# Weights transposed back in 32x32 blocks by VectorE, and plain transfers in place of DMA transposes, in an agent-attention kernel with a gated convolution

## The chip, the core and the metric

The kernel runs on one core of a Trainium2 chip. The metric is the device time of one execution in microseconds. Five engines work side by side, each with its own queue of instructions in program order: TensorE (PE, with weight loads as PEld), VectorE (DVE), ScalarE (ACT), GpSimd (POOL) and SyncE (SP), which here issues nearly all transfers. The transfers run on 16 DMA engines.

## What is computed

For each of 4 batches q, k and v are 12,800 x 128 and there are 49 agents of 128. Two softmaxes compose into an attention, and a gated causal convolution with two projections follows:

```
def sm(a, b):
    s = scale * (a @ b.transpose(0, 2, 1))
    s = s - s.max(-1, keepdims=True)
    e = np.exp(s)
    return e / (e.sum(-1, keepdims=True) + 1e-09)
a2k = sm(agents, k)
agent_v = a2k @ v
q2a = sm(q, agents)
x = q2a @ agent_v
...
for k in range(K):                       # K = 5 taps, causal
    gate_pre += conv_w[k][None, None, :] * xp[:, k:k + S, :]
gate = 1.0 / (1.0 + np.exp(-gate_pre))
val = x @ w_val
return (gate * val @ w_out).astype(np.float32)
```

## The kernel before

The attention's result x is never formed. Since x is the 49 weights of a position (q2a) times the 49 rows of agent_v, the kernel folds agent_v into the convolution's taps and into w_val once for each batch (`fold_weights`), and the gate and the value then are matmuls over the 49 weights of a position and its four predecessors. The weights and the folded matrices are each split into a high and a low half-precision part; the products high x high, high x low and low x high need 49 x 3 = 147 rows of contraction. 128 of them form the tile x1 (low, high and 30 agents' high once more), and the 19 that are left, for each of 5 taps, form the 95 rows of x2.

The work is cut into units of 1,280 positions: 10 a batch, 40 in all, and for the convolution into 100 chunks of 512 positions (the last is cut into 384 and 128). The steps are named by letters:

- k (`key_scores`, L406): scores of a unit of keys against the agents, 8 matmuls of 320 columns, a copy to ks, a running maximum.
- v (`agent_values`, L475): the exponentials, their 32x32 block transposes on VectorE (L400), and the product with v, added up in PSUM over the 10 units of a batch.
- max and fold: the maximum over a batch's keys (L433), and the folded weights (L527), in 2 and 5 pieces.
- q (`queries`, L743): scores of a unit of queries, block transposes into sT (L400), maximum (L757), subtraction (L762), exponential (L770), sum (L775), division (L783). The weights w of a unit lie in qw with 128 positions on the partitions, 10 blocks of 49 agents. They are split into pt (10 blocks of 128 columns): high by a cast on ACT (L790), 30 high ones copied once more by POOL in two strided pieces (L796), low by a subtraction on POOL (L804).
- t (`transposes`, L837): pt has positions on its partitions, x1 needs them along its free dimension. For the first 4 units PE transposes 10 blocks and ACT and DVE copy them out (L859 to L871). For the other 36, one DMA transpose a unit does it (L845). Then `shifts` (L876) fills x2 by plain transfers from x1: each row of x1 is copied to 5 rows of x2, shifted by one position each. From unit 4 on this is done once for a pair of units, in two transfers by `X2CUTS` (L37): 16 rows of x1 (50, 53, ...) to 80 rows of x2, and 3 rows to 15 (L894). `halo` (L823) copies four columns between segments on POOL.
- g, a, o (`gates` L908, `values` L952, `project` L991): for each chunk 6 matmuls for the gate (L932 over x1, L936 over x2) and tanh, 2 for the value (L959, L963) and the product with the gate, and 3 for the projection (L1004 to L1006), scaled on ACT and sent out by pairs of chunks (L1040).

Buffers: 11 load slots for k, q and v (NLOAD), 4 tiles of pt, 4 of x1 with one pair of units each, 3 of x2, one PSUM bank each for gate, value and projection.

The order on PE is written out by hand (`order`, L1107). All other engines, SP among them, follow a planner (`Plan`, L70): each step has an engine, a cost in us, and, for a transfer, the time that it takes of the wire; the planner runs the steps in a model and emits them in the order of their start. Loads are held back to 20 us ahead of their use. A step waits by keys that it reads and writes, such as ("pt", 2, 0) or ("x1", 1, 0). A transfer that waits holds up every later one on SP.

Of the kernel before, what the change touches and what calls it, by code (L numbers as in the profile page):

```python
# [9 lines left out]
F32 = mybir.dt.float32  # L10
F16 = mybir.dt.float16
# [6 lines left out]
P = 128  # L18
G = 4
# [13 lines left out]
NDUP = 30  # L33
THIRDS = 16
X2R = 19
LAST = 42
X2CUTS = ((0, THIRDS, 1, 3, 0.5), (THIRDS, X2R, LAST, 3, 0.2))  # L37
# [4 lines left out]
NPT = 4  # L42
NX = 4
# [147 lines left out]
def tile_agent_attention_gated_conv(  # L191
# [37 lines left out]
    sts = ring(2, [P, NBLK, AP_], F32, "sT")  # L229
    qmx = ring(2, [P, NBLK], F32, "qmx")  # L230
# [3 lines left out]
    pts = ring(NPT, [P, NBLK, P], F16, "pt")  # L234
# [198 lines left out]
    def key_max(b):  # L433
# [16 lines left out]
        def spread():  # L450
            nc.vector.tensor_reduce(
                out=mrow, in_=p1[0:2, 0:P].rearrange("j (g a) -> j a g", g=G),
                axis=AX.X, op=ALU.max,
            )
            nc.vector.tensor_copy(
                out=mrep, in_=mrow.unsqueeze(1).to_broadcast([2, G, BLK])
            )

        add("dve", 0.5, spread, [at1], ["mrep"])
# [67 lines left out]
    def fold_weights(b):  # L527
# [58 lines left out]
        ghi = wst[:, 0:TAPS, 0:A]  # L586
        vhi = wst[:, TAPS, 0:A]

        def thirds(x, first, end):
            return x[..., first:end:3]  # L590

        def lows(low, full, hi, less):


            for out, first, end in zip(low, (2, 0, 1, LAST), (A, LAST, A, A)):
                less(out, thirds(full, first, end), thirds(hi, first, end))

        def rest(out, full, s, hi):
            dve.scalar_tensor_tensor(
                out=out, in0=full, scalar=rs[:, s : s + 1], in1=hi,  # L600
                op0=ALU.mult, op1=ALU.subtract,
            )

        def val_weights():
# [9 lines left out]
            dve.tensor_scalar_mul(vhi, pv[:, 0:A], rs[:, 1:2])  # L614
            low = (
                wst[:, TAPS, 2 * A : 2 * A + THIRDS], wst[:, TAPS, 2 * A + THIRDS :],
                x2v[:, HALO, 0:THIRDS], x2v[:, HALO, THIRDS:],
            )
            lows(low, pv[:, 0:A], vhi, lambda out, full, hi: rest(out, full, 1, hi))

        gate_lows = (
            wst[:, 0:TAPS, 2 * A : 2 * A + THIRDS], wst[:, 0:TAPS, 2 * A + THIRDS :],
            x2g[:, :, 0:THIRDS], x2g[:, :, THIRDS:],
        )

        def gate_weights():
            dve.tensor_scalar_mul(ghi, gw, rs[:, 0:1])
# [6 lines left out]
        def gate_rest_pool():  # L634
# [3 lines left out]
            lows(gate_lows, gs, ghi, less)  # L638

        def gate_rest():  # L640
            lows(gate_lows, gw, ghi, lambda out, full, hi: rest(out, full, 0, hi))
# [9 lines left out]
        add("dve", 1.58, val_weights, [at_v], [(*w_, "v"), "mxv"])  # L651
        add(
            "act", 0.4,
            lambda: nc.scalar.copy(out=wst[:, 0:TAPS, A : 2 * A], in_=ghi),
            [(*w_, "g")], [(*w_, "d")],
        )
        add(
            "act", 0.22, lambda: nc.scalar.copy(out=wst[:, TAPS, A : 2 * A], in_=vhi),
            [(*w_, "v")], [(*w_, "e")],
        )  # L660
        if b:
            add("dve", 0.95, gate_rest, ["gw", (*w_, "g")], [(*w_, "r")])
# [4 lines left out]
        def transposes():  # L667
# [6 lines left out]
            "pe", 0.6, transposes, [(*w_, n) for n in "derv"] + [(*w_, "g")], [at_w],  # L674
# [530 lines left out]
```

## Time and profile before

| | us |
|---|---|
| median of 3 runs | 418.15 |
| lowest and highest | 415.93, 419.5 |
| the profiled execution, its own time | 415.52 |
| its span, first to last instruction | 413.4 |

| engine | busy us | share | instructions |
|---|---|---|---|
| PE | 395.0 | 96% | 3905 |
| DVE | 256.0 | 62% | 489 |
| ACT | 297.8 | 72% | 519 |
| POOL | 282.1 | 68% | 381 |

A busy share is an average over the whole span. A row of a group names its line, engine and operation, what it writes and reads, then its count, its busy time and the mean of one. A row of the transfers names what is written from what, the engine that issues, how often, the size of one (KB are 1,024 bytes here) and the median time from issue to landing, where it is known. The share of the DMA engines is the time that their packets took, over 16 engines; it can pass 1, since a packet's time counts in the window in which it starts. The GB/s count each packet once.

### The profile page before, as it was taken

Reading aid. Unit: us, or ns where it says so; the run is one execution under the profiler, and the core shown is the slowest. Engines: PE = TensorE matmul, PEld = TensorE weight load, DVE = VectorE, ACT = ScalarE, POOL = GpSimd, SP = SyncE. Lnnn points to the kernel's source line nnn. Section 1 sums busy time; section 2 is a strip of 40 time slices with the busy share of each in tenths; the row PEclk is TensorE's granted clock in tenths of the full one; section 3 lists DMA queues with packets and bytes.
Section 4 is the critical chain, followed back from the end, with each engine's and each line's share of the span. In section 5 each row is a group of like instructions: output and inputs, shape, how many; then the busy total and the mean of one; then the engine's idle time right before and its main releaser. Section 6 shows DMA issues by size and latency. Waiting matters only on the chain.

```text
span 413.4 us, 10115 instructions
## 1 busy us (share of the span) xinstructions
PE 395.0 (96%) x3905; PEld 197.1 (48%) x3905; DVE 256.0 (62%) x489; ACT 297.8 (72%) x519; POOL 282.1 (68%) x381
## 2 busy tenths in 40 slices
PE   4859999999999999999999999999999999999996
PEld 2348544445555434445446544445465544444443
DVE  3758688854835857566745687576664697643231
ACT  2564568597884777869885677689886676888875
POOL 1003679766878698656788775896578789998752
PEclk9969999999999999999999999999999999999999
DMA  8999999999999999999999999999999999999933
GB/s 323 420 416 411 366 360 357 284 358 252 350 320 267 336 269 317 337 306 330 346 356 296 298 347 311 340 303 342 310 348 313 261 302 291 223 251 232 216 144 138
DMA packets 75130, 127.63 MB, mean 309 GB/s; under 512 B 50466, under 2 KB 50850, under 8 KB 75084
## 3 DMA queue, kind: packets, MB, share of 16 engines
q1 hardware_dynamic: 74940, 126.87, 99.9%
q8 instruction: 30, 0.49, 0.5%
q10 hardware_dynamic: 144, 0.13, 0.2%
q14 instruction: 16, 0.13, 0.1%
HBM read 79.25 MB, written 26.21 MB: 255 GB/s over the span
## 4 chain that ended last, share of the span: by engine, by line
PE 85%; DMA 7%; ACT 3%; DVE 3%; POOL 1%; issue 1%; SPq 0%; DVEq 0%; ACTq 0%
PE gate L932 25%; PE sc L390 17%; PE av L494 11%; PE out L1004 5%; PE val L959 5%; PE gate L936 5%; PE val L963 5%; PE out L1005 5%; PE out L1006 5%; DMA ld<-kT 4%; DMA x<-x 2%; ACT e L485 1%; ACT th L945 1%; PE sc L859 1%; DVE h L972 0%
## 5 line engine op out<-in xcount | busy, mean ns | idle before, releaser
L985 POOL TENSOR_TENSOR hl<-h,hh 128x512 f16<-128x512 f32 x99 | 114.6, 1160 | 57.4 <-ACT hh L980 55.0
L932 PE MATMUL gate<-x,stat 128*128 128x512 f16 (+1 forms) x500 | 124.3, 378 | 0.6 <-ACT e L485 0.4
L972 DVE SCALAR_TENSOR_TENSOR h<-th,val 128x512 f32<-128x512 f32 x100 | 68.1, 681 | 81.6 <-PE out L1005 27.8
L390 PE MATMUL sc<-ld,ag_sb 128*32 128x320 f32 x1280 | 97.1, 442 | 7.5 <-DMA ld<-kT 6.3
L1025 ACT ACTIVATE ob<-out,oscale 128x512 f32<-128x512 f32 x98 | 67.2, 686 | 23.4 <-PE out L1006 23.3
L945 ACT ACTIVATE th<-gate,unscale 128x512 f32<-128x512 f32 x100 | 68.5, 685 | 21.3 <-PE gate L936 19.2
L932 PEld LDWEIGHTS <-stat 128*128 128x128 f16 x505 | 47.7, 97 | 60.6 <-issue 5.5
L980 ACT CAST hh<-h 128x512 f16<-128x512 f32 x99 | 60.7, 613 | 14.4 <-DVE h L972 13.8
L762 POOL TENSOR_TENSOR qw<-sT,qmx 128x490 f32<-128x490 f32 x40 | 40.5, 1018 | 43.8 <-DVE qmx L757 41.3
L390 PEld LDWEIGHTS sc<-ld,ag_sb 128*32 128x32 f32 x1280 | 37.9, 111 | 54.9 <-issue 17.4
L494 PE MATMUL av<-ld,eT 128*32 128x129 f32 (+1 forms) x1400 | 50.5, 277 | 2.2 <-DVE eT L400 2.2
L494 PEld LDWEIGHTS av<-ld,eT 128*32 128x32 f32 (+1 forms) x1400 | 45.6, 115 | 10.3 <-issue 3.4
L416 ACT COPY ks<-sc 128x640 f32<-128x640 f32 x40 | 27.6, 693 | 27.3 <-PE sc L390 25.1
L400 DVE STREAM_TRANSPOSE sT<-sc 128x640 f32<-128x640 f32 x40 | 33.5, 842 | 19.9 <-PE sc L390 19.1
L400 DVE STREAM_TRANSPOSE eT<-e 128x640 f32<-128x640 f32 x40 | 33.5, 839 | 19.1 <-ACT e L485 11.2
L804 POOL TENSOR_TENSOR pt<-qw,pt 128x490 f16<-128x490 f32 x40 | 43.9, 1104 | 1.9 <-ACT pt L790 1.8
L485 ACT ACTIVATE e<-ks,kbias 128x320 f32<-128x320 f32 x80 | 39.4, 554 | 7.4 <-DVE eT L400 4.6
L783 POOL TENSOR_TENSOR qw<-qw,qr 128x490 f32<-128x490 f32 x40 | 40.3, 1009 | 3.3
L936 PE MATMUL gate<-x,stat 95*128 95x512 f16 x100 | 38.0, 380 | 0.8 <-DMA x<-x 0.8
L959 PE MATMUL val<-x,stat 128*128 128x512 f16 x100 | 38.0, 380 | 0.1
L425 DVE TENSOR_REDUCE kmx<-ks 128x2 f32<-128x640 f32 x39 | 31.5, 811 | 10.5 <-ACT ks L416 10.5
L963 PE MATMUL val<-x,stat 95*128 95x512 f16 x100 | 38.0, 380 | 0.0
(133 smaller groups left out, 407.7 us busy)
## 6 DMA issues: line engine op xcount, KB each, us to landing
ld<-kT SPq DMA_DIRECT2D x40, 640.0 KB, 7.0
ld<-qT SPq DMA_DIRECT2D x40, 640.0 KB, 9.1
ld<-vP SPq DMA_DIRECT2D x39, 645.0 KB, 6.5
outT<-ob SPq DMA_DIRECT2D x48, 512.0 KB, 7.2
x<-x SPq DMA_DIRECT2D x18, 400.0 KB, 5.2
x<-x SPq DMA_DIRECT2D x18, 75.0 KB
x<-x SPq DMA_DIRECT2D x4, 200.0 KB
outT<-ob SPq DMA_DIRECT2D x3, 256.0 KB
```

Source lines behind the costliest of these rows:

```text
L390: nc.tensor.matmul(out=out[g * BLK : (g + 1) * BLK, j, 0:GT], lhsT=ag_sb[:, b, j * BLK : (j + 1) * BLK], rhs=src[:, g * GT : (g + 1) * GT] ...
L400: nc.vector.transpose(out=out.rearrange("p n (j i) -> p j n i", j=2), in_=in_.rearrange("p j (n i) -> p j n i", i=BLK),)
L494: nc.tensor.matmul(out=av[o + j : o + j + cols, 0 : C + 1], lhsT=et[:, n, j : j + cols], rhs=vt[:, n, :], start=(u == 0 and n < 2), stop=( ...
L932: nc.tensor.matmul(out=pg, lhsT=stat[:, k, :], rhs=x1[:, c : c + w], start=(k == 0), stop=False,)
L936: nc.tensor.matmul(out=pg, lhsT=stat[0 : TAPS * X2R, TAPS + 1, :], rhs=x2[0 : TAPS * X2R, o2 : o2 + w], start=False, stop=True,)
L945: lambda: nc.scalar.activation(out=th, in_=pg, func=AF.Tanh, scale=unscale[:, 0:1]),
L959: nc.tensor.matmul(out=pv, lhsT=stat[:, TAPS, :], rhs=x1s[(b * NCH + n0 // CH) // 5 % NX][:, PAD + o2 : PAD + o2 + w], start=True, stop=False,
L963: nc.tensor.matmul(out=pv, lhsT=stat[0 : TAPS * X2R, TAPS + 2, :], rhs=x2[0 : TAPS * X2R, o2 : o2 + w], start=False, stop=True,)
L972: lambda: nc.vector.scalar_tensor_tensor(out=h, in0=th, scalar=1.0, in1=pv, op0=ALU.add, op1=ALU.mult),
L980: "act", 0.18 + 0.43 * scale, lambda: nc.scalar.copy(out=hh, in_=h),
L985: lambda: nc.gpsimd.tensor_tensor(out=hl, in0=h, in1=hh, op=ALU.subtract),
L1025: lambda: nc.scalar.activation(out=ob[:, o : o + w], in_=po, func=AF.Copy, scale=oscale if w == CH else 1.0),
```

## The change

Weights are no longer split with positions on the partitions. VectorE first transposes w back in 32x32 blocks (`back`): two overlapping groups of 32 agents, 0 to 31 and 17 to 48 (SLOT = 17), 640 elements a partition into the new tile wT, in which a partition is one of 32 agents in one of four strips of positions. ACT casts wT to the high parts and POOL subtracts, both 640 wide, into the tile pr, which holds four kinds of rows (low, high, high, low) for a pair of units. Then `strips` moves pr to x1 by plain transfers, eight for a pair of units: for each of the four strips of 32 partitions one transfer of 30 partitions with 3 rows each to 90 rows of x1, and one of 19 partitions with 2 rows each to 38 rows. A row has 640 elements of 2 bytes. The host lays q out so that each strip is a run of 640 positions. The first four units stay on PE, with pt now lying inside pr.

x1's rows are so ordered anew (triples for 30 agents, pairs for 19), and the folded weights follow (`highs`, `lows`): for all batches the gate's splits are now on ACT and POOL, where before this held for batch 0 and the others had them on DVE. x2 takes other rows: `X2CUTS` now sends 17 rows of x1 to 85 rows of x2 and 2 rows to 10. The copy of the keys' maximum and the unscaling go from DVE to ACT. The hand-written order on PE is new; its start is shown, and the number of steps of each kind is the same.

```
-NDUP = 30
-THIRDS = 16
+SLOT = 17
+AFIRST = 30
 X2R = 19
-LAST = 42
-X2CUTS = ((0, THIRDS, 1, 3, 0.5), (THIRDS, X2R, LAST, 3, 0.2))
+X2CUTS = ((0, SLOT, 1, 3, 0.5), (SLOT, X2R, 124, 2, 0.2))
...
+NPR = 2
...
+    wts = ring(2, [P, 2, GT], F32, "wT")
...
-    pts = ring(NPT, [P, NBLK, P], F16, "pt")
+    prs = ring(NPR, [P, 4, 2 * GT], F16, "pr")
...
-        add("dve", 0.5, spread, [at1], ["mrep"])
+            ),
+            [at1], ["mrow"],
+        )
+        add(
+            "act", 0.25,
...
+        def highs(i, full, copy):
+            for out, agents in (
+                (wst[:, i, 0 : 3 * AFIRST].rearrange("p (a k) -> p a k", k=3)[:, :, 0:2], full[:, 0:AFIRST]),
+                (wst[:, i, 3 * AFIRST :].rearrange("p (a k) -> p a k", k=2), full[:, AFIRST:]),
+            ):
+                copy(out, agents.unsqueeze(2).to_broadcast([P, agents.shape[1], 2]))
+
+        def lows(x2, k, full, less):
+
+
+            one, two = wst[:, k, 0 : 3 * AFIRST : 3], wst[:, k, 3 * AFIRST :: 2]
+            for out, first, end in (
+                (wst[:, k, 2 : 2 + 3 * (AFIRST - SLOT) : 3], SLOT, AFIRST),
+                (wst[:, k, 2 + 3 * (AFIRST - SLOT) : 3 * AFIRST : 3], AFIRST, A - 2),
+                (x2[..., 0:SLOT], 0, SLOT), (x2[..., SLOT:], A - 2, A),
+            ):
+                hi = one[..., first:end] if end <= AFIRST else two[..., first - AFIRST : end - AFIRST]
+                less(out, full[..., first:end], hi)
...
-        if b == 0:
-            add("pool", 0.47, gate_scaled, ["gw", "rsg"], ["gs"])
-            add("act", 0.4, lambda: nc.scalar.copy(out=ghi, in_=gs), ["gs"], [(*w_, "g")])
-            add("pool", 1.27, gate_rest_pool, ["gs", (*w_, "g")], [(*w_, "r")])
-        else:
-            add("dve", 0.47, gate_weights, ["gw", "rsg"], [(*w_, "g")])
...
+        add("pool", 0.47, gate_scaled, ["gw", "rsg"], ["gs"])
+        add(
+            "act", 0.4,
+            lambda: nc.scalar.copy(
+                out=wst[:, 0:TAPS, 0 : 3 * AFIRST].rearrange("p t (a k) -> p t a k", k=3)[..., 0:2],
+                in_=gs[:, :, 0:AFIRST].unsqueeze(3).to_broadcast([P, TAPS, AFIRST, 2]),
+            ),
+            ["gs"], [(*w_, "g")],
+        )
+        add(
+            "act", 0.35,
+            lambda: nc.scalar.copy(
+                out=wst[:, 0:TAPS, 3 * AFIRST :].rearrange("p t (a k) -> p t a k", k=2),
+                in_=gs[:, :, AFIRST:].unsqueeze(3).to_broadcast([P, TAPS, A - AFIRST, 2]),
+            ),
+            ["gs"], [(*w_, "d")],
+        )
+        add("pool", 1.27, gate_rest, ["gs", (*w_, "g"), (*w_, "d")], [(*w_, "r")])
...
-        add("dve", 0.15, unscales_, ["mxg", "mxv"], [("unscale", x)])
+        add(
+            "act", 0.22,
...
+        if on_pe(b, u):
+            pt = blocks(g)
...
+            p_ = [("pr", i_, k, n) for k in (2 * h, 2 * h + 1) for n in range(2)]
+            add("act", 0.8, high, [("qw", g % NPT)], [p_[0]])
+            add("pool", 0.7, again, [("qw", g % NPT)], [p_[1], p_[2]])
+            add("pool", 1.3, low, [("qw", g % NPT), p_[0]], [p_[3]])
...
+        pr = prs[i_][:, :, h * GT : (h + 1) * GT]
+        wT = wts[x]
+
+        def back():
+            pairs = [summed.ap[0], summed.ap[1], (SLOT, 2), (1, BLK)]
+            nc.vector.transpose(
+                out=wT.rearrange("p j (n i) -> p n j i", i=BLK),
+                in_=bass.AP(summed.tensor, summed.offset, pairs),
+            )
+
+        add("dve", 0.83, back, [("qw", g % NPT)], [("wT", x)])
+        add(
+            "act", 0.69, lambda: nc.scalar.copy(out=pr[:, 1:3], in_=wT),
+            [("wT", x)], [("pr", i_, k, h) for k in (1, 2)],
+        )
+        add(
+            "pool", 1.43,
             lambda: nc.gpsimd.tensor_tensor(
-                out=pt[:, :, 0:A], in0=w, in1=pt[:, :, A : 2 * A], op=ALU.subtract
-            ),
-            [("qw", g % NPT), (*p_, 0)], [(*p_, 1)],
-        )
+                out=pr[:, 0::3], in0=wT, in1=pr[:, 1:3], op=ALU.subtract
+            ),
+            [("wT", x)] + [("pr", i_, k, h) for k in (1, 2)], [("pr", i_, k, h) for k in (0, 3)],
...
-        return [(x, i, h) for h in halves for x in ("x1", "x1b")] + [("x1h", i)] * (0 in halves)
+        return [(x, i, h) for h in halves for x in ROWS] + [("x1h", i)] * (0 in halves)
...
+    ROWS = ("x1", "x1b", "x1c", "x1d")
+
+    def strips(g):
+
+
+        i, s = g // 2 % NPR, g // 2 % NX
+        pr, x1 = prs[i], x1s[s]
+        step = pr.ap[0][0]
+        for part, (slots, a0, a1, row) in enumerate(
+            (((0, 1, 2), 0, AFIRST, 0), ((2, 3), AFIRST - SLOT, BLK, 3 * AFIRST))
+        ):
+            n, rows = len(slots), len(slots) * (a1 - a0)
+            for strip in range(G):
+                src = pr[strip * BLK + a0 : strip * BLK + a1, slots[0] : slots[-1] + 1]
+                dst = x1[row : row + rows, PAD + strip * 2 * GT : PAD + (strip + 1) * 2 * GT]
+                add(
+                    "dma", 0.6,
+                    lambda src=src, dst=dst: nc.sync.dma_start(out=dst, in_=src),
+                    [("pr", i, k, h) for k in slots for h in range(2)],
+                    [(ROWS[2 * part + strip % 2], s, strip // 2)], rows * 0.0053,
+                )
...
-            dst = unit_rows(g)
-            add(
-                "dma", 1.4,
-                lambda: nc.sync.dma_start_transpose(
-                    out=dst.rearrange("p (n i) -> p n i", i=P),
-                    in_=pt.rearrange("p n r -> p (n r)"),
-                ),
-                [(*p_, n) for n in range(3)], [("x1", g // 2 % NX, g % 2)], 2.4,
-            )
-            shifts(b, u)
+            if g % 2:
+                strips(g)
+                shifts(b, u)
...
-            first += A
...
-        "k0.4 k0.1 k0.7 k0.9 k0.5 k0.0 k0.8 k0.6 k0.2 k0.3 m0 m0 v0.0 v0.1 v0.2 q0.0 v0.3 v0.4 "
-        "v0.5 v0.6 q0.1 v0.7 v0.8 v0.9 f0 t0.0 f0 k1.2 k1.0 k1.4 q0.2 f0 k1.3 f0 t0.1 g0 f0 q0.3 "
...
+        "k0.4 k0.0 k0.3 k0.1 k0.8 k0.2 k0.6 k0.5 k0.7 k0.9 m0 m0 q0.0 v0.0 v0.1 v0.2 v0.3 v0.4 "
+        "v0.5 v0.6 v0.7 v0.8 q0.1 v0.9 k1.4 t0.0 f0 k1.2 f0 q0.2 k1.3 k1.0 f0 t0.1 f0 g0 a0 q0.3 "
+        "q0.5 f0 g1 o0 k1.5 k1.1 a1 t0.2 g2 t0.4 a2 q0.4 t0.3 g3 o1 a3 g4 a4 o2 t0.5 q0.7 q0.6 o3 "
...
+    qT = np.ascontiguousarray(
+        q.reshape(b, nu // 2, G, 2, GT, c).transpose(0, 5, 1, 3, 2, 4).reshape(b, c, n)
+    )
```

More of the change, by code (lines that the diff above doesn't have):

```diff
@@ L585, in fold_weights, with rest @@
         x2v = wst[:, TAPS + 2, 0 : TAPS * X2R].rearrange("p (r k) -> p k r", k=TAPS)
[L586 to L598, printed above, removed]
+        def highs(i, full, copy):
[13 more added lines that the diff above has]
+                less(out, full[..., first:end], hi)
+        def rest(out, full, hi):
             dve.scalar_tensor_tensor(
-                out=out, in0=full, scalar=rs[:, s : s + 1], in1=hi,
+                out=out, in0=full, scalar=rs[:, 1:2], in1=hi,
                 op0=ALU.mult, op1=ALU.subtract,
@@ L613, in val_weights @@
             dve.reciprocal(out=rs[:, 1:2], in_=mx[:, 1:2])
[L614 to L627, printed above, removed]
+            highs(TAPS, pv[:, 0:A], lambda out, full: dve.tensor_scalar_mul(out, full, rs[:, 1:2]))
+            lows(x2v[:, HALO], TAPS, pv[:, 0:A], rest)
         def gate_scaled():
@@ L673, in fold_weights @@
         add(
-            "pe", 0.6, transposes, [(*w_, n) for n in "derv"] + [(*w_, "g")], [at_w],
+            "pe", 0.6, transposes, [(*w_, n) for n in "dgrv"], [at_w],
             key="m",
@@ L787, in queries, with high, again @@
         add("pool", 1.29, weigh, [("qw", g % NPT), ("qr", x)], [("qw", g % NPT), ("qr", x)])
-        p_ = ("pt", g % NPT)
-        add(
-            "act", 0.6, lambda: nc.scalar.copy(out=pt[:, :, A : 2 * A], in_=w),
-            [("qw", g % NPT)], [(*p_, 0)],
-        )
-        def again():
-            for o, end, first, last in ((2 * A, 2 * A + THIRDS, 2, A), (2 * A + THIRDS, P, 0, LAST)):
+        h = g % 2
+        i_ = g // 2 % NPR
+        if on_pe(b, u):
+            pt = blocks(g)
+            own = pt[:, :, 0 : 3 * AFIRST].rearrange("p n (a k) -> p n a k", k=3)
+            far = pt[:, :, 3 * AFIRST :].rearrange("p n (a k) -> p n a k", k=2)
+            def high():
+                nc.scalar.copy(out=own[..., 1], in_=w[:, :, 0:AFIRST])
+                nc.scalar.copy(out=far[..., 0], in_=w[:, :, AFIRST:])
+            def again():
@@ L796, in again, with low @@
                 nc.gpsimd.tensor_scalar(
-                    out=pt[:, :, o:end], in0=w[:, :, first:last:3],
+                    out=own[..., 2], in0=w[:, :, SLOT : SLOT + AFIRST],
                     scalar1=1.0, scalar2=0.0, op0=ALU.mult, op1=ALU.add,
                 )
-        add("pool", 0.76, again, [("qw", g % NPT)], [(*p_, 2)])
-        add(
-            "pool", 1.09,
+            def low():
+                for out, agents, hi in (
+                    (own[..., 0], w[:, :, 0:AFIRST], own[..., 1]),
+                    (far[..., 1], w[:, :, AFIRST:], far[..., 0]),
+                ):
+                    nc.gpsimd.tensor_tensor(out=out, in0=agents, in1=hi, op=ALU.subtract)
@@ L862, in matmuls @@
                 )
-        add("pe", 0.65, matmuls, [("pt", g % NPT, n) for n in range(3)], [at], key="t")
+        i, s, h = g // 2 % NPR, g // 2 % NX, g % 2
+        add(
+            "pe", 0.65, matmuls, [("pr", i, k, n) for k in (2 * h, 2 * h + 1) for n in range(2)],
+            [at], key="t",
+        )
         add(
             "act", 0.69, lambda: nc.scalar.copy(out=dst[:, 0], in_=ps[:, 0, 0 : HB * P]),
-            [at], [("x1", g // 2 % NX, g % 2)],
+            [at], [(x, s, h) for x in ROWS if x != "x1b"],
         )
```

49 lines of the change are left out of this document (23 added, 26 removed), and 43 rows, old and new, of the table order.

## The prediction

> **What bounds the kernel now.** I read the page first, then the windows by stage, then who TensorE (PE) waited for.
>
> ```profile
> PE 395.0 (96%) x3905; PEld 197.1 (48%) x3905; DVE 256.0 (62%) x489; ACT 297.8 (72%) x519; POOL 282.1 (68%) x381
> ```
>
> The windows: start and end, length, busy us of PE, weight loads, DVE, ACT and POOL, then the granted clock, the DMA share and GB/s.
>
> ```profile
> core 0 of [0], span 413.4 us
> 6.00:20.00 14.00, 12.25 (x148) 5.09 (x144) 8.91 (x18) 5.89 (x9) 0.00 (x0) 1.00 1.02 422
> 54.00:400.00 346.00, 344.49 (x3335) 167.02 (x3328) 218.41 (x404) 263.15 (x459) 264.68 (x348) 1.00 1.04 303
> ```
>
> What PE waited for, us in total, times, longest:
>
> ```profile
> PE sc L390 <- DMA ld<-kT: 6.3, 3, 5.7
> PE av L494 <- DVE eT L400: 2.2, 1, 2.2
> ...
> PE gate L936 <- DMA x<-x: 0.8, 1, 0.8
> ...
> PE val L578 <- DVE avT L550: 0.5, 1, 0.5
> PE out L536 <- DVE av L533: 0.4, 1, 0.4
> ```
>
> PE sets the end: from 54 to 400 us it stands still for 346.00 - 344.49 = 1.5 us in all, at full clock. No other engine is above 72%. The transfers are the second resource: a share of 1.04 says that the 16 DMA engines nearly always have a packet, yet in the whole run PE waits for the shift into x2 once, for 0.8 us. The idle that is left lies before 54 us: the wait for the first key load (5.7 of the 6.3), 2.2 us ahead of v0.0 (L494), 0.4 and 0.5 us in the first fold (L536, L578).
>
> The change leaves PE's matmuls as they are (same units on PE, same 8 transposes per fold, same chunks). So it can win little: these last 3.1 us and the 1.5 us above. It can lose much, by making PE wait.
>
> **The change part by part: the engines.**
>
> The instructions that write pt (ns: least, median, most), and the two 640-wide rows nearest to what is added:
>
> ```profile
> L796 POOL TENSOR_SCALAR pt<-qw x80: 366/398/433, 39.8 to 385.6; 128x160 f16<-128x160 f32 x40, 128x140 f16<-128x140 f32 x40
> L790 ACT CAST pt<-qw x40: 585/602/608, 39.7 to 383.4; 128x490 f16<-128x490 f32 x40
> L804 POOL TENSOR_TENSOR pt<-qw,pt x40: 1092/1104/1127, 40.5 to 384.1; 128x490 f16<-128x490 f32 x40
> ...
> L845 SPq DMA_TRANSPOSE x<-pt x36: 1334/3230/8020, 72.3 to 386.0; - x36
> ```
>
> ```profile
> L400 DVE STREAM_TRANSPOSE sT<-sc 128x640 f32<-128x640 f32 x40 | 33.5, 842 | 19.9 <-PE sc L390 19.1 <-POOL qw L762 0.8
> ...
> L416 ACT COPY ks<-sc 128x640 f32<-128x640 f32 x40 | 27.6, 693 | 27.3 <-PE sc L390 25.1 <-DVE kmx L425 1.8
> ```
>
> For each of 36 units DVE gains one 640-wide block transpose, 0.84 us as in L400: 30 us, DVE to 286. ACT's cast grows from 490 to 640 elements, 0.60 to at most the 0.69 of L416: +3.3 us. POOL loses two L796 and one L804 (1.90 us) and gains one 640-wide subtraction, 1.10 x 640/490 = 1.44 us: -16 us. On a unit's chain from weights to x1 that is 0.84 + 0.69 + 1.44 = 2.97 against 0.60 + 1.10 = 1.70 us, so it is 1.3 us later. In the fold three gate splits go from DVE to POOL (a handful of operations of at most L796's size, 2 us in all, each), and the copy of mrow and the unscaling go to ACT (tiny operands, within one L790 of 0.6 us either way, four times). All of this lies under PE now and under the transfers below; I count it as nothing. Without that cover only the 4 folds would show, 2 us each at most.
>
> The new order puts q0.0 ahead of v0.0, k1.4 ahead of the first fold step and k1.2 inside it: that is 1.1 us of work (one unit's scores) in the 2.2 us hole, and the 0.4 and 0.5 us holes filled, some 2 us. It counts only while PE is the bound.
>
> **The transfers.** What the issue list says of before:
>
> ```profile
> DMA packets 75130, 127.63 MB, mean 309 GB/s; under 512 B 50466, under 2 KB 50850, under 8 KB 75084
> ```
>
> ```profile
> ld<-kT SPq DMA_DIRECT2D x40, 640.0 KB, 7.0
> ld<-qT SPq DMA_DIRECT2D x40, 640.0 KB, 9.1
> ld<-vP SPq DMA_DIRECT2D x39, 645.0 KB, 6.5
> outT<-ob SPq DMA_DIRECT2D x48, 512.0 KB, 7.2
> x<-x SPq DMA_DIRECT2D x18, 400.0 KB, 5.2
> x<-x SPq DMA_DIRECT2D x18, 75.0 KB
> x<-x SPq DMA_DIRECT2D x4, 200.0 KB
> outT<-ob SPq DMA_DIRECT2D x3, 256.0 KB
> ld<-vP SPq DMA_DIRECT2D x2, 322.5 KB
> x<-pt SPq DMA_TRANSPOSE x36, 11.7
> ob<-moe SPq DMA_DIRECT2D x1, 261.0 KB
> outT<-ob SPq DMA_DIRECT2D x1, 192.0 KB
> x<-x SPq DMA_DIRECT2D x4, 37.5 KB
> ag_sb<-agT ACTq DMA_DIRECT2D x1, 128.0 KB
> outT<-ob SPq DMA_DIRECT2D x1, 64.0 KB
> ```
>
> and one lone DMA transpose, in the window from 386.9 to 388.9 us:
>
> ```profile
> DMA packets 1337, 0.43 MB, mean 215 GB/s; under 512 B 1312, under 2 KB 1312, under 8 KB 1337
> ```
>
> The list has 256 transfers: 36 transposes and 220 plain ones. A transpose of 327,680 bytes in packets of 256 leaves 1,280 of them; the window has 1,312 under 512 B, so 32 tiny ones close it, two for each of 16 engines. The page has 50,466; less 36 x 1,312 = 47,232 that is 3,234 for the plain ones. With one from each of 16 engines they would have 220 x 16 = 3,520. Missing are 286 = 22 x 13. There are 22 of just one odd kind: the second shift into x2, 3 partitions of x1 times 5 taps into 15 rows (18 of 75 KB, 4 of 37.5 KB). So **these ran on 3 engines, 5 rows each**, where the first shift (16 partitions, 80 rows) and the 128-partition ones ran on 16. Fifteen rows could have gone to 15 engines; they went to 3, in equal shares that divide the first dimension of both sides.
>
> Now the change's shapes. The first shift becomes 17 partitions to 85 rows. The strips come in two parts: 30 partitions to 90 rows, and 19 partitions to 38 rows. Equal shares that divide both: 15 engines for 30 and 90. For 17 and 85, and for 19 and 38, there is no number from 2 to 16: **one engine**. The other bound is an uneven split over 16, at most 2 partitions each (10 rows, 2 us). I take one engine, since no transfer of the 256 has an uneven share. The Trainium skill, page "DMA: Bandwidth & Descriptors", section "Why a DMA increments its semaphore by 16 and not by 1", speaks against this change: a hardware-queue transfer runs on the largest count up to 16 that divides both sides' slowest dimension (100 partitions 10, 127 one), on the lowest-numbered engines. The trace's 3-engine shift agrees; by that rule the sum is the one below, by an uneven split it is rival B. Which engine is not in the trace; I take the same one each time.
>
> Price on that first engine:
>
> ```profile
> HBM read 79.25 MB, written 26.21 MB: 255 GB/s over the span
> ```
>
> From the 6 to 20 us row an engine moves 422/16/1.02 = 25.9 GB/s, 0.198 us for a row of 5,120 B.
> - Loads and outputs: (79.25 + 26.21)/16 = 6.59 MB, 254 us. Unchanged.
> - First shift: 18 x 85 x 5,120 B and 4 x 85 x 2,560 B = 8.70 MB on one engine: 336 us, 16.8 us a pair (5 rows or 1 us before).
> - Second shift, 2 partitions to 10 rows, two engines: 0.51 MB each, 20 us.
> - Strips of 90 rows on 15 engines: 72 x 6 rows x 1,280 B: 21 us.
> - Strips of 38 rows on one: 72 x 38 x 1,280 B = 3.50 MB: 135 us by the rate. The upper bound is the lone transpose's window: 2,000 ns x 16 engines / 1,337 packets = 24 ns for 256 B, 14 more than the rate. That gives 63 instead of 49 ns a row, 173 us. I take 145, as the excess of a plain 5,120 B row is nil.
> - Removed: 36 transposes, at most 2 us of every engine each.
>
> Sum **776 us** (766 to 804): 39 us a pair of units where PE needs 413/20 = 20.6. The first engine takes its share of each load in the order of issue, so every load behind a shift lands when that engine is done; PE waits, 11 loads deep.
>
> Around it: a shift can't be issued before its strips have landed, and SP, which issues in order, holds the loads and outputs behind that wait. From issue to first packet:
>
> ```profile
> 389.43 1.48 SPq L894 DMA_DIRECT2D x<-x  x2
> ```
>
> ```profile
> DMA  9899200000989997997349456952999859977754
> ```
>
> That is 389.4 to 394.4 us in 40 slices: packets resume at slice 10, 1.2 us after the issue. 18 x 1.2 = 22 us if nothing else is queued on the engine; 0 if always something is, 45 if the strips' own issue shows as well. From the last landing (some 3.5 us after 389.43) to the end at 413.4 are 20 us, start 1.2. SP itself: 144 strips at the 0.73 us of a shift are 105 us, the 36 transposes, by the L845 row above, 36 x 3.23 = 116. Even, and not the bound.
>
> ```profile
> L894 SPq DMA_DIRECT2D x<-x x44: 612/732/859, 45.2 to 390.1; - x44
> ```
>
> Span: 1.2 + 776 + 22 + 20 = 819 us; the profiled execution took 415.52 us for a span of 413.4, so 821; the runs' median, 418.15, is 2.6 above it: **824 us**. Bounds: 766 + 21 = 787, less what overlaps the ends, say 760; above, 804 + 45 + 21 = 870, and up to 5 us a pair where the engine stands idle because PE has not freed load buffers: 960.
>
> **Rivals.**
> A, the forecast: one engine, 824 us. Chance 0.85.
> B, not slower: transfers split unevenly over 16, place the 17-partition shift and the 19-partition strips, 2 us and 0.2 us instead of 16.8 and 2. It decides as soon as a shift lands within the few us of now: PE stays the bound, the start wins 2 us, 416 us, at the best 413. For it: the program text asks for nothing odd. Against it: the 286. Chance 0.10, a quarter of that beyond 1% faster.
> C: one engine, but a different one in turn. Then no engine is overfull (254 + 512/16 + 22 is about 308 us), and only the shift's landing is 13 us later, each pair. Today's slack for it is unknown, 0 to 13 us; half of it, 18 x 6.5 = 117, gives 535. Against it: nothing seen for it. Chance 0.03.
> D: the engine idles longer than I allow, SP's order holding loads behind outputs that wait for PE: two pair times in series, (39 + 20.6) x 18 pairs + some 70 for start and end, 1,140. Chance 0.02.
>
> **How the numbers follow.** 760 to 960 holds A nine times in ten, 0.77, near 8 in 10, and leaves B, C and D out, which lie far off. One per cent is about what a measurement of this kernel tells from no change. Faster by over 1%: 0.03 (B's quarter). Within 1%: 0.07. Slower: 0.90.
>
> **What would show it.** Right: PE busy near 395 us but under half of the span; PE's waits led by DMA, the shift (gate L936's line) and the loads; the first shift, 425 KB, landing 17 us or more after issue; the mean DMA share near 0.4, with PE idle. In a window with only a 17-partition shift the share is 1/16. Wrong: a shift that lands in 5 us, or a PE share above 90%. If the shift takes 17 us but the span is near 535, the engine was not the same each time; if strips land at once and only the shift is slow, the 135 to 173 us fall away.

## The result, and the profile after

| | before | after |
|---|---|---|
| median of 6 runs | 418.82 us (415.93 to 423.67) | 842.02 us (840.81 to 844.71) |
| profiled execution | 415.52 us, span 413.4 | 844.71 us, span 842.9 |
| ratio | | 2.012, 95% interval 2.003 to 2.022 |

The changed kernel takes twice the time. The page's rows of busy time and of packets:

```profile
PE 448.3 (53%) x3905; PEld 209.6 (25%) x3905; DVE 275.8 (33%) x506; ACT 309.8 (37%) x530; POOL 272.1 (32%) x324
...
DMA packets 37918, 127.66 MB, mean 151 GB/s; under 512 B 4035, under 2 KB 13635, under 8 KB 37869
```

No engine is above 53%, and as many bytes as before move at half the rate. Who TensorE (PE) waited for (us in total, times, longest):

```profile
PE gate L988 <- DMA x<-x: 362.2, 22, 30.5
PE out L1058 <- POOL hl L1037: 12.3, 6, 5.9
PE sc L391 <- DMA ld<-kT: 7.2, 6, 5.8
PE gate L984 <- DMA x<-pr: 2.7, 1, 2.7
```

One row holds it: 22 waits for the shift into x2, 362.2 us, where before there was one of 0.8. The windows (start, end, length, busy of PE, weight loads, DVE, ACT and POOL, granted clock, DMA share, GB/s), first nearly the whole run, then three short stretches of one pair of units:

```profile
54.00:800.00 746.00, 386.25 (x3303) 176.97 (x3304) 236.82 (x420) 267.98 (x456) 250.40 (x287) 0.75 0.43 139
```

```profile
299.00:303.00 4.00, 2.04 (x10) 0.71 (x8) 2.26 (x3) 1.85 (x3) 2.46 (x4) 1.00 0.06 26
315.00:322.00 7.00, 0.22 (x1) 0.13 (x2) 0.00 (x0) 0.00 (x0) 0.00 (x0) 0.50 0.06 26
323.00:327.00 4.00, 4.00 (x11) 1.47 (x10) 1.49 (x3) 1.92 (x4) 0.90 (x1) 0.50 0.06 24
```

0.06 is 1/16: in all three stretches one engine of 16 works. In the first two it carries the rows of the 17-partition shift at 26 GB/s, in the third the 38-row strips of the next pair at 24. In the second, PE, DVE, ACT and POOL all stand still until PE's last 0.22 us. The same stretch in the timeline of SP and of PE:

```profile
298.91 4.01 SPq L946 DMA_DIRECT2D x<-x  x1
302.97 1.48 SPq L384 DMA_DIRECT2D ld<-kT  x1
304.50 1.50 SPq L1092 DMA_DIRECT2D outT<-ob  x1
306.04 19.13 SPq L889 DMA_DIRECT2D x<-pr  x8
```

```profile
321.78 0.61 PE L988 MATMUL gate<-x,stat 95*128 95x512 f16 x1 [20.74 <-DMA x<-x]
```

PE waits 20.74 us for the shift and then runs at half clock (granted clock 0.50 in the windows above). The row at 298.91 is the small second shift, of 10 rows; by the trace's records the one of 85 rows was issued at 291.74 and landed at 320.76. SP, meanwhile, spends 19.13 us on eight strips, and goes on with the next only as older transfers land. SP's own waits:

```profile
SPq L889 <- DMA x<-x: 100.1, 21, 8.2
SPq L946 <- DMA x<-pr: 92.1, 27, 5.7
```

The second row is the true dependency, a shift behind its strips. The first is not one: no strip reads or overwrites what the shift before it writes. The strips wait for it nevertheless, because this program lets only eight transfers be under way at once (the planner has a constant for it, LANES = 8). The trace's records show it: every transfer that SP issues tells of its landing by one of eight semaphores, in strict turn, so an issue has to wait until the transfer eight places before it has landed. In the stretch above four strips go out, and the fifth starts at 320.78 us, just after the 85-row shift, eight places before it, has landed.

**How many engines a transfer had can be counted.** The row "under 512 B" counts, beside the 256-byte packets of the DMA transposes, one tiny closing packet for each engine of each plain transfer. The changed kernel's list of issues has 176 transfers that run on 16 engines (loads, outputs and constants), 22 first shifts, 22 second ones and 72 strips of each kind. With the forecast's 1, 2, 15 and 1 engines that makes 176 x 16 + 22 + 44 + 72 x 15 + 72 = 4,034; the page has 4,035. The Trainium skill's page "DMA: Bandwidth & Descriptors", section "Why a DMA increments its semaphore by 16 and not by 1", gives the rule behind it (the largest number up to 16 that divides the slowest dimension of both sides, on the lowest-numbered engines); this trace agrees with the number of engines.

### The profile page after: what moved, and what is told of

It is laid out like the page before. It is cut to its first block, busy times and chain, and to the rows that moved or that the text cites. A ratio compares the mean times of both kernels' runs of the same rounds, so it can differ in the third digit from the quotient of the medians.

```text
span 842.9 us, 10251 instructions
## 1 busy us (share of the span) xinstructions
PE 448.3 (53%) x3905; PEld 209.6 (25%) x3905; DVE 275.8 (33%) x506; ACT 309.8 (37%) x530; POOL 272.1 (32%) x324
## 4 chain that ended last, share of the span: by engine, by line
DMA 79%; PE 11%; SPq 6%; POOL 1%; ACT 1%; DVE 1%; issue 1%; POOLq 0%; DVEq 0%; ACTq 0%
DMA x<-x 22%; DMA x<-pr 18%; DMA outT<-ob 17%; DMA ld<-qT 9%; DMA ld<-kT 8%; DMA ld<-vP 5%; SPq L946 3%; PE gate L984 3%; SPq L384 2%; PE av L498 2%; PE sc L391 2%; PE gate L988 1%; PE val L1011 1%; PE out L1058 1%; POOL hl L1037 1%; PE val L1015 1%
## 5 line engine op out<-in xcount | busy, mean ns | idle before, releaser
L988 PE MATMUL gate<-x,stat 95*128 95x512 f16 x100 | 44.3, 443 | 362.2 <-DMA x<-x 362.2
L984 PE MATMUL gate<-x,stat 128*128 128x512 f16 (+1 forms) x500 | 136.2, 406 | 3.8 <-DMA x<-pr 2.7
L391 PE MATMUL sc<-ld,ag_sb 128*32 128x320 f32 x1280 | 105.1, 465 | 7.7 <-DMA ld<-kT 7.2
L988 PEld LDWEIGHTS <-stat 95*128 95x128 f16 x101 | 10.4, 103 | 380.2 <-DMA x<-x 369.6
L832 POOL TENSOR_TENSOR pr<-wT,pr 128x640 f16<-128x640 f32 x36 | 50.4, 1403 | 30.9 <-ACT pr L827 30.8
L498 PE MATMUL av<-ld,eT 128*32 128x129 f32 (+1 forms) x1400 | 55.3, 294 | 2.0 <-DMA ld<-vP 1.8
L1058 PE MATMUL out<-hl,wo 128*128 128x512 f16 x98 | 41.1, 419 | 12.3 <-POOL hl L1037 12.3
L1011 PE MATMUL val<-x,stat 128*128 128x512 f16 x100 | 43.8, 438 | 0.0
L1015 PE MATMUL val<-x,stat 95*128 95x512 f16 x100 | 43.4, 434 | 0.0
L1056 PE MATMUL out<-hh,wo 128*128 128x512 f16 x98 | 41.8, 426 | 0.0
```

The lines of the kernel that those rows point to most:

```text
L391: nc.tensor.matmul(out=out[g * BLK : (g + 1) * BLK, j, 0:GT], lhsT=ag_sb[:, b, j * BLK : (j + 1) * BLK], rhs=src[:, g * GT : (g + 1) * GT] ...
L498: nc.tensor.matmul(out=av[o + j : o + j + cols, 0 : C + 1], lhsT=et[:, n, j : j + cols], rhs=vt[:, n, :], start=(u == 0 and n < 2), stop=( ...
L984: nc.tensor.matmul(out=pg, lhsT=stat[:, k, :], rhs=x1[:, c : c + w], start=(k == 0), stop=False,)
L988: nc.tensor.matmul(out=pg, lhsT=stat[0 : TAPS * X2R, TAPS + 1, :], rhs=x2[0 : TAPS * X2R, o2 : o2 + w], start=False, stop=True,)
L1011: nc.tensor.matmul(out=pv, lhsT=stat[:, TAPS, :], rhs=x1s[(b * NCH + n0 // CH) // 5 % NX][:, PAD + o2 : PAD + o2 + w], start=True, stop=False,
L1015: nc.tensor.matmul(out=pv, lhsT=stat[0 : TAPS * X2R, TAPS + 2, :], rhs=x2[0 : TAPS * X2R, o2 : o2 + w], start=False, stop=True,)
```

## The experiments

The kernel before ran beside each batch (medians 417.9 to 420.4). There are twelve kernels, in four groups. A time without a range is that of one run.

**1. One cut each.** The first shift cut in two:

```diff
-X2CUTS = ((0, SLOT, 1, 3, 0.5), (SLOT, X2R, 124, 2, 0.2))
+X2CUTS = ((0, 16, 1, 3, 0.5), (16, SLOT, 49, 3, 0.1), (SLOT, X2R, 124, 2, 0.2))
```

> The kernel after the change, with the first shift cut in two: 16 partitions to 80 rows, and the 17th partition to its 5 rows by itself; the strips stay as they are. One-engine theory (a transfer runs on the largest number of engines up to 16 that divides the first dimension of both sides, always the same first engine; its work is the time): the 336 us of the 17-partition shift become 22 (5 rows a pair instead of 85, at 0.198 us) plus at most 22 for the lone partition, so the engine's sum falls from 776 to 462 to 484; with the 67 us by which the measured span (842.9) exceeded the 776, 529 to 551 us, and the strips of 38 rows are what still holds PE up. Queue theory (SP, which issues in order, and the longer chain VectorE - ScalarE - GpSimd ahead of each strip hold the loads back; the engines are idle because nothing is issued): nothing that it names is taken away, and SP gets 22 more issues, so 830 to 870 us.

534.88 us. Its packets, and PE's longest wait:

```profile
DMA packets 38358, 127.66 MB, mean 240 GB/s; under 512 B 4475, under 2 KB 14075, under 8 KB 38309
```

```profile
PE gate L988 <- DMA x<-x: 61.5, 15, 7.4
```

309.8 us come back for 292 to 314 expected, with 22 transfers more on SP: the queue theory falls as the cause of the main loss. The closing packets are 440 more, 22 x (16 + 5 - 1): the 16 partitions ran on 16 engines, and the lone partition with its 5 rows on 5, not on one.

The strips cut instead, the shift left:

```diff
-            (((0, 1, 2), 0, AFIRST, 0), ((2, 3), AFIRST - SLOT, BLK, 3 * AFIRST))
+            (
+                ((0, 1, 2), 0, AFIRST, 0), ((2, 3), AFIRST - SLOT, BLK - 3, 3 * AFIRST),
+                ((2, 3), BLK - 3, BLK, P - 6),
+            )
...
-    ROWS = ("x1", "x1b", "x1c", "x1d")
+    ROWS = ("x1", "x1b", "x1c", "x1d", "x1e", "x1f")
```

> The kernel after the change, with the strips of 19 partitions (38 rows) cut into 16 partitions (32 rows) and 3 partitions (6 rows); the 17-partition shift stays. One-engine theory: the 145 us of the 38-row strips on the first engine become 2 rows each at 0.05 us, twice, 72 times: 14; sum 645, with the 67 us left over 712 us. Queue theory: SP gets 72 more issues of 0.7 us, 50 us, and is later with every load: 880 to 900 us. If the shift alone were the cause and the strips cost nothing, 840.

780.98 us. 63.7 us come back, half of the 131 expected; the packets under 512 B are 5,330 = 176 x 16 + 22 x 3 + 72 x (15 + 16 + 3), so the cut did what it should, and the shift still holds PE:

```profile
PE gate L991 <- DMA x<-x: 314.3, 22, 25.5
```

Both cuts together:

> The kernel after the change with both cuts: shifts of 16, 1 and 2 partitions, strips of 30, 16 and 3. No transfer of any size is left on one engine. One-engine theory: the first engine's sum is 254 for loads and outputs, 22 to 44 for the first shift, 20 for the second, 21 for the strips of 90 rows and 14 for the rest, 331 to 353 us, below PE's 395; PE is the bound again and the time is that of before, 413 to 425 us. Queue theory: SP has 94 more issues than in the changed kernel, 66 us, and the longer chain is still there: above 700 us.

495.44 us (491.48 to 501.01), ratio 1.178, interval 1.171 to 1.185. **Both theories miss.** No transfer is on one engine any more (closing packets 5,770 = 176 x 16 + 22 x 23 + 72 x 34), the share of DMA and the waits are these, and yet 75 us are missing:

```profile
PE 422.3 (85%) x3905; PEld 204.0 (41%) x3905; DVE 276.8 (56%) x506; ACT 308.1 (62%) x530; POOL 272.1 (55%) x324
```

```profile
54.00:480.00 426.00, 367.62 (x3329) 173.65 (x3328) 239.29 (x422) 270.66 (x464) 253.85 (x290) 0.93 0.76 247
```

```profile
PE gate L991 <- DMA x<-x: 49.7, 13, 9.8
PE sc L391 <- DMA ld<-kT: 8.0, 4, 5.8
```

What the time stands on: the span of this execution is 497.5 us, 84 more than before; PE waits 49.7 us for the shift, and its own busy time is 27.3 above that of before, at a clock of 0.93. PE is busy for 85% at most, and the 16 DMA engines for 76%. They even run dry: by the trace's packets, from 54 us to 20 us before the end no packet was in flight for 31 us, where it was 4 us in the kernel before.

**2. The divisor by itself.** Eighteen partitions to 90 rows, one to 5:

```diff
-X2CUTS = ((0, SLOT, 1, 3, 0.5), (SLOT, X2R, 124, 2, 0.2))
+X2CUTS = ((0, 18, 1, 3, 0.5), (18, X2R, 126, 2, 0.2))
```

> The kernel after the change, but the first shift takes 18 partitions to 90 rows and the second one partition to 5 rows; one agent's row of x2 then holds another agent's weights, so the values of that agent are not the reference's. It moves no fewer bytes and issues no fewer transfers than the changed kernel. One-engine theory, with equal shares that divide both sides: 18 and 90 go on 9 engines, 10 rows each, 2 us instead of 16.8, 40 us in all instead of 336; the sum is 776 - 336 + 40 + at most 2 = 480, with the 67 us 525 to 550 us. A rule by size (a transfer of over 80 rows, or one that isn't a multiple of 16 partitions, is slow) gives no gain, 830 to 870 us; so does the queue theory.

534.21 us, where the changed kernel took 844.71 with 17 partitions, the same transfers in number and no fewer bytes. One partition more makes the kernel 310 us faster. Its packets:

```profile
DMA packets 38159, 127.66 MB, mean 240 GB/s; under 512 B 4276, under 2 KB 13876, under 8 KB 38110
```

4,276 is 176 x 16 + 22 x (9 + 5) + 72 x 16 exactly: nine engines for 18 and 90, where 16, 15 or 10 would each have shown.

The 17-partition shift in the kernel before, without strips, block transposes or a new order:

```diff
-X2CUTS = ((0, THIRDS, 1, 3, 0.5), (THIRDS, X2R, LAST, 3, 0.2))
+X2CUTS = ((0, 17, 1, 3, 0.5), (17, X2R, 45, 3, 0.2))
```

> The kernel before the change, DMA transposes and all, with one edit: its first shift takes 17 partitions to 85 rows instead of 16 to 80, and its second 2 instead of 3; one agent's row of x2 then holds another's weights, so that agent's values are not the reference's. No strip, no block transpose, no new order. One-engine theory: the first engine's sum is 254 for loads and outputs, 336 for the shift, 20 for the second shift, 71 for the transposes, 681; with 43 (the ends) to 67 us (what the changed kernel showed) on top, 725 to 750 us. If the strips or the longer chain were needed for the loss, a kernel without them stays below 450 us.

726.76 us: one number makes 307 us of the loss by itself.

```profile
DMA packets 74778, 127.62 MB, mean 176 GB/s; under 512 B 50114, under 2 KB 50498, under 8 KB 74732
```

```profile
PE gate L936 <- DMA x<-x: 258.5, 21, 23.3
PE sc L390 <- DMA ld<-kT: 7.4, 2, 6.0
```

50,114 is 36 x 1,312 for the transposes + 176 x 16 + 22 x (1 + 2), exactly.

**3. Where the 75 us of the kernel with both cuts are.** Its strips on three queues:

```diff
-                add(
-                    "dma", 0.6,
-                    lambda src=src, dst=dst: nc.sync.dma_start(out=dst, in_=src),
+                who, queue = (("dma", nc.sync), ("act", nc.scalar), ("pool", nc.gpsimd))[part]
+                add(
+                    who, 0.6,
+                    lambda src=src, dst=dst, queue=queue: queue.dma_start(out=dst, in_=src),
```

> The kernel with both cuts (495 us), the same transfers, but the strips of 16 partitions are issued on ScalarE's queue and those of 3 on GpSimd's, so that SP issues 4 strips a pair of units instead of 12. Issue theory (what is left in that kernel is SP's issuing: 12 x 0.75 = 9 us between the second unit's weights and the shift, where one transpose took 3.2, so the shift lands some 6 us late and PE waits 49.7 us for it, at a lower clock after each hole): SP has 3 us left ahead of the shift, PE's wait for the shift falls below 10 us, 420 to 440 us, as long as ScalarE (308 busy + 72 x 0.4 to 0.75) stays below PE. Chain theory (the 1.3 us longer way through VectorE, ScalarE and GpSimd and the strips' small rows make the shift late, whoever issues them): 480 to 500 us.

505.96 us (503.52 to 507.73), ratio 1.206, interval 1.198 to 1.214. Not faster. Who issues the strips (ns: least, median, most), and PE's wait:

```profile
L893 SPq DMA_DIRECT2D x<-pr x72: 851/894/1607, 78.1 to 478.3; - x72
L893 ACTq DMA_DIRECT2D x<-pr x72: 575/583/1722, 79.1 to 477.4; - x72
L893 POOL DMA_DIRECT2D x<-pr x72: 552/572/747, 79.3 to 478.2; - x72
```

```profile
PE gate L992 <- DMA x<-x: 53.1, 13, 9.7
```

A third of the strips is left on SP, and the wait is as long as it was. The same page of the Trainium skill, section "Rules for kernel authors", says that spreading transfers over the issuers saves issue time only, since all share the same 16 engines; here it did not save any of the whole. With only the strips of 3 partitions moved, to ScalarE:

```diff
+                who, queue = (("dma", nc.sync), ("dma", nc.sync), ("act", nc.scalar))[part]
```

> The kernel with both cuts, but only the strips of 3 partitions leave SP, for ScalarE's queue: SP issues 8 strips a pair, as in the changed kernel. Issue theory: 3 us a pair come back of the 6 that are late, so about half of the 75 us lost, 455 to 475 us. Chain theory: 480 to 500 us.

508.52 us, the same. So the issue theory in this form is wrong: moving strips off SP does not bring the 75 us back. (ScalarE and GpSimd then issue them, among their own work.)

Next, eight idle transfers in the kernel before, first in the way of the shift:

```diff
+            for j in range(8 * (g % 2)):
+                add(
+                    "dma", 0.6,
+                    lambda j=j: nc.sync.dma_start(out=spare[0:30, j], in_=pt[0:30, 0, 0:32]),
+                    [(*p_, n) for n in range(3)], [("spare", j)], 0.05,
+                )
...
-        src = row_keys(s, range(0, g % 2 + 1))
+        src = row_keys(s, range(0, g % 2 + 1)) + [("spare", j) for j in range(8)]
```

> The kernel before the change, with eight idle transfers (30 rows of 64 bytes each, from pt into a spare tile that nothing reads) issued on SP between the second transpose of each pair and its shift, which waits for them too: 8 x 0.75 = 6 us more ahead of the shift, and hardly a byte. Nothing else is changed; the result is the same. Issue theory: before loses what the kernel with both cuts loses, 470 to 500 us. Chain theory: SP's issues cost nothing as long as SP is not full (276 us of issuing and 108 more, of 413), 416 to 425 us.

515.80 us (513.38 to 518.83), ratio 1.228, interval 1.218 to 1.237: 96 us for 144 transfers that carry 0.28 MB, more than the theory gave.

```profile
PE gate L943 <- DMA x<-x: 65.9, 18, 7.7
PE sc L391 <- DMA ld<-kT: 6.0, 1, 6.0
```

The same eight behind the shift, which no longer waits for them:

```diff
+        if not on_pe(b, u):
+            for j in range(8):
+                add(
+                    "dma", 0.6,
+                    lambda j=j: nc.sync.dma_start(out=spare[0:30, j], in_=pts[g % NPT][0:30, 0, 0:32]),
+                    [("pt", g % NPT, n) for n in range(3)] + [("x2", s % 3, o, r0)], [("spare", j)], 0.05,
+                )
```

> The kernel before the change with the same eight idle transfers a pair of units (30 rows of 64 bytes, from pt into a spare tile that nothing reads) as in the run that took 516 us, but placed behind the pair's shift in SP's order, with no one waiting for them; there they had stood between the second transpose and the shift, which waited for them. The result is the same. Way theory (what costs is the time that they add between a pair's weights and its shift, since PE's gate waits at the end of that way): moved out of the way they cost little, 416 to 435 us. Resource theory (SP's issues, the transfers that may be under way at once, or the 16 engines' time for small packets are the limit): as dear as before, 490 to 520 us.

488.18 us (485.90 to 490.01), ratio 1.161, interval 1.156 to 1.167. The way theory's 416 to 435 is far off, and the resource theory's 490 to 520 is just missed. Of 96 us, 69 stay where the shift does not wait for the transfers. They are not out of everyone's way, though, as they were meant to be: they read the pt that GpSimd's subtraction (L805) writes again four units later, and GpSimd waits for them. So the two theories are not cleanly parted here.

```profile
POOL pt L805 <- DMA spare<-pt: 20.7, 8, 4.8
```

Their cost on SP beside that of shifts and transposes, and what they waited for there:

```profile
L905 SPq DMA_DIRECT2D spare<-pt x144: 779/780/1496, 87.9 to 472.0; - x144
```

```profile
L895 SPq DMA_DIRECT2D x<-x x44: 618/749/942, 46.7 to 463.9; - x44
L846 SPq DMA_TRANSPOSE x<-pt x36: 1358/2490/6951, 73.8 to 457.0; - x36
```

```profile
SPq L905 <- DMA ld<-vP: 5.8, 7, 1.7
SPq L905 <- DMA ld<-qT: 5.3, 6, 1.9
SPq L905 <- DMA x<-x: 5.0, 8, 1.0
SPq L905 <- DMA outT<-ob: 3.1, 5, 1.2
SPq L905 <- DMA ld<-kT: 2.2, 4, 1.0
```

Added up record by record, since the medians hide the long ones, SP issues idle transfers for 124 us, transposes for 96, loads and outputs for 99 and shifts for 32: 352 of 488. Beside it stand the 21 us of the last rows, all of them waits for the transfer eight places before. From 54 us to 20 us before the end, SP's queue is taken for 94% (it issues, waits for the transfer eight places before, or has a gap of under 0.1 us between two instructions), against 85% in the kernel before. So SP is nearly full. These transfers stand ahead of the next pair's transposes in SP's order, and PE's wait for the shift is again the longest:

```profile
PE gate L944 <- DMA x<-x: 39.2, 13, 8.8
```

**4. The way from weights to gate, in the kernel with both cuts.** Each shift made to wait only for the strips that it reads:

```diff
-                src, [("x2", s % 3, o + i * UNIT, r0) for i in range(n)], us * n
+                [k for k in src if g < PE_FIRST or k[0] in ("x1h",) + (("x1e", "x1f") if r0 == SLOT else ("x1", "x1b"))],
+                [("x2", s % 3, o + i * UNIT, r0) for i in range(n)], us * n
```

> The kernel with both cuts (495 us), all transfers on SP, but each shift waits only for the strips whose rows it reads: the 16-partition shift and the lone partition for the four strips of 30 partitions, the last shift for the strips of 3; so the first shift can be issued after 4 strips of a pair instead of 12, some 8 x 0.75 = 6 us earlier, and no engine gets more work. Latency theory (each pair's gate waits for the way weights - strips - shift, 28.3 us from the start of the second unit's last subtraction to the gate's last matmul in the kernel with both cuts against 22.2 in the kernel before, and the next pair's weights stand in the engines' queues behind that gate's chunks; with three queues this way was down to 20.0, but ScalarE and GpSimd, which now issued strips, brought the weights 9 us later): the way falls to about 22, PE's wait for the shift from 49.7 us to below 12, and the time to 416 to 435 us. Bandwidth theory (the strips' 1,280-byte rows and the shift share the engines with loads, whatever the order): 480 to 500 us.

503.69 us (500.01 to 505.50), ratio 1.203, interval 1.197 to 1.209. (The way in that text is a mean over the 18 pairs, from start times in the timeline.) The wait fell as expected, the time did not. PE's waits, then GpSimd's:

```profile
PE out L1062 <- POOL hl L1041: 26.5, 9, 5.8
PE val L1015 <- DVE h L1028: 11.7, 3, 9.5
PE gate L992 <- DMA x<-x: 7.6, 5, 4.6
```

```profile
POOL x L864 <- DMA x<-pr: 98.9, 12, 14.8
POOL hl L1041 <- ACT hh L1036: 43.8, 40, 4.7
```

The stall changed its place: GpSimd stands 98.9 us at the halo copy of L864, which needs strips of all three kinds (the six of the pair's second half), and hl and the next weights stand behind it. In the kernel before, the same copy (L829) waited 4.2 us in all. The scores and strips of all units from the eleventh on, 5 places earlier in PE's order:

```diff
+    names = order.split()
+
+    def early(n, x):
+        late = x[0] in "qt" and int(x[1]) * NU + int(x[3]) >= 10
+        return n - 5 * late
+
+    order = " ".join(x for _, x in sorted(enumerate(names), key=lambda p: (early(*p), p[0])))
```

> The kernel with both cuts, with the scores and strips of every unit from the eleventh on moved 5 places ahead in the list that sets PE's order (a pair of units has some 23 places there, 20 us): the weights start some 4 us earlier for each gate. Latency theory: of the 4 us a pair that are lost, half or more come back, 425 to 465 us. Bandwidth theory: 485 to 500 us.

513.14 us (511.83 to 514.88), ratio 1.227, interval 1.219 to 1.235: slower than with both cuts alone, and the wait for the shift stays (52.6 us, 10 times). Last, early shifts and the planner's costs nearer to the measured ones:

```diff
-LAND = 1.4
+LAND = 2.4
...
-                    "dma", 0.6,
+                    "dma", 0.87,
```

> The kernel with both cuts and early shifts (504 us), with two numbers of the planner changed that orders each engine's instructions: a strip's issue costs 0.87 us there instead of 0.6, and a landing 2.4 instead of 1.4. Same instructions, same transfers, other orders. In that kernel PE's wait for the shift had fallen from 49.7 to 7.6 us, but the time had not: GpSimd now stood 98.9 us, in 12 stretches of up to 14.8, at the copy of four columns from the pair before (the halo), which waits for all 12 strips, and the products hl and the next weights stood behind it. Order theory (what is lost is no resource: the orders of the in-order engines were made for transfers that come sooner than they do, and whoever waits for a late strip holds up what stands behind it): GpSimd's wait at the halo copy below 40 us, 425 to 465 us. Resource theory (SP's 216 strips and 66 shifts, or the 16 engines, are the limit, in whatever order): 490 to 510 us.

495.09 us (492.18 to 499.74), ratio 1.182, interval 1.175 to 1.188. GpSimd's wait at the halo copy fell to about what was expected; the time went back only to that of both cuts:

```profile
POOL hl L1041 <- ACT hh L1036: 75.7, 48, 5.3
POOL x L864 <- DMA x<-pr: 40.3, 10, 7.2
```

```profile
PE gate L992 <- DMA x<-x: 28.0, 11, 4.8
PE sc L391 <- DMA ld<-kT: 7.3, 7, 5.8
```

No version beat the kernel before.

## Why the prediction was right, and where it was not

- **One engine for 17 and 85, 19 and 38: right.** The closing packets give the number of engines of every kind of transfer, exactly in most of the runs and within one in the others, and 18 partitions for 17 gives back 310 us. Rival B, the uneven split, falls with the share of 0.06.
- **The same engine each time: right as far as the time tells.** Rival C had 535 us for a new engine each time; the trace does not name engines, but the loads' 254 us are in the sum only if the shift shares their engine, and the sum holds. Rival D (1,140 us) falls with the time too.
- **The price of the shift: right.** 26 GB/s in the window of the shift for 25.9 foreseen; 29.0 us from issue to landing in the stretch shown, for 17 or more; 309.8 us back for the cut, 310.5 with 18 partitions, 307 lost in the kernel before, for 336 - 22 at most.
- **The price of the 38-row strips: right by the row, not by the whole.** 24 GB/s in their window is 53 ns a row, the 145 us of the sum. Cutting them gave back 64 us, not 131, but brought 72 transfers more, and the engines ran dry: by the trace's packets, from 1.2 us to some 20 us before the end none was in flight for 31 us, against 3 us in the changed kernel. That is 28 of the missing 67 us; the rest is not accounted for.
- **The sum and what lies around it: 24 us short.** Span 819 foreseen, 842.9 measured. The end was right: PE's last wait for a shift ends at 823.35, 19.6 us before the end for 20 foreseen.

```profile
823.35 0.61 PE L988 MATMUL gate<-x,stat 95*128 95x512 f16 x1 [18.02 <-DMA x<-x]
```

  So from 1.2 to 823.35 us are 822 us for 776 of work, 46 more, where 22 were taken for gaps between strips and shift. The total is near, but the term is not what was meant by it: by the trace's packets, in only 2.8 of these 822 us was no packet in flight, so something was nearly always queued, the case for which the forecast had 0. What is short is the work. The 5,120-byte packets took 0.245 us in the mean of the run (median 0.196), for 0.198 in the sum. That those of the first engine were the longer ones is inferred, since the trace does not name engines.
- **"Even, and not the bound", of SP: the weak step.** The forecast compared SP's 105 us of strips with 116 of transposes and dropped the subject. As issuing this was near: added up, 144 strips take 122 us in the kernel with the shift cut, and 36 transposes 136 in the kernel before. Left out was the wait for the transfer eight places before: 84 us in that kernel, 35 in the one before. In the changed kernel the one engine hides what this costs. With both cuts, which bring 94 transfers more, SP's queue is taken for 97% between 54 us and 20 us before the end, and 75 us of loss remain, at transfers that are each wide enough.
- **PE busy near 395, under half of the span: wrong.** It is 448.3, 53%, at a mean granted clock of 0.75 in the long window. In the window from 315 to 322 the clock is 0.50, and the gate's row took 0.61 us for 0.38 before. The Trainium skill's page "TensorE: Matmul & The Clock Gate", section "Part 1: The HAM clock gate (the "warmup" mystery)", says that an idle array is throttled to half the clock and released after some microseconds of work; the trace agrees. It cost little here, since the first engine set the pace; in the kernel with both cuts PE's longer busy time is 27 of the 84 us of the profiled execution.
- **Cover for the engines' work, the start: nothing seen against them.** The 2 us at the start are lost in the rest.

**What stays open** is why the kernel with both cuts takes 495 us. Shown: 144 small transfers more on SP cost the kernel before 69 us behind the shift, and 96 in its way, with PE, DVE, ACT, POOL and the 16 DMA engines below full; in the long stretch no packet was in flight for 41 and 67 us. What is nearly full is SP's queue, by the count above: 85% before, 97% with both cuts, 96% and 94% with the idle transfers, 97% with the planner's costs. That makes SP the likeliest limit of these kernels. It is not shown as the only one: with three queues SP is down to about 68%, and the time is 506 us. Shown not to be the cause by themselves: the strips' place on SP (three queues, 506 us), PE's wait for the shift (7.6 us left, 504), the lead of the scores (513), the planner's costs (495). Each time the stall moved to another in-order queue. Argued, and not shown: that SP's issues, the bound of eight transfers under way and the queues' fixed orders together make the loss. A kernel with as many bytes in fewer, wider strips would tell; a strip that takes several groups of partitions at once wasn't tried.

## What to carry to other kernels

Before a partition count is changed, take the first dimension (of more than one) of both sides of each transfer and look for the largest number up to 16 that divides both: 16 to 17 partitions took a transfer from 16 engines to one, and the kernel from 420 to 727 us. The number can be read off afterwards, since each engine of a transfer leaves one tiny packet. And count transfers, not only bytes: in a kernel whose queues are ordered by hand or by a planner, eight more small ones a pair of units cost 3.8 to 5.3 us of its 20.6 (69 and 96 us over 18 pairs). No engine was full in the profile; that SP's queue was shows only when its issues and waits are added up one by one, not from counts and medians.

## What the runs showed of the hardware that was not expected

- A lone partition read for 5 taps into 5 rows ran on 5 engines (440 = 22 x (16 + 5 - 1) closing packets more), so a dimension of one is passed over.
- A transfer of 30 rows of 64 bytes takes SP 0.78 us to issue, twice the 0.38 of a load of some 640 KB (the median of the loads of values in the kernel with both cuts):

```profile
L384 SPq DMA_DIRECT2D ld<-vP x41: 327/382/1956, 10.4 to 369.0; - x41
```

- Issued from ScalarE or GpSimd, a strip took that queue 0.57 to 0.58 us (0.73 for the strips of 3 on ScalarE), time that ScalarE and GpSimd need for the weights of the next pair.
